# Experts' rests at fixed column counts in place of a choice among arms, in an attention, expert and dense kernel on one core

## The chip, the cores and the metric

One Trainium2 chip, one of its cores. The time is that of one execution of the program on the device, in microseconds. Of several runs the median is given. The engines are called as the profile calls them: PE (TensorE) for matrix products, PEld for its loading of weights, DVE (VectorE), ACT (ScalarE), POOL (GpSimd) and SP (SyncE, which issues most transfers). [...]

## What is computed

Three layers one after the other, in float32, on 2 x 768 tokens of 512 features:

```python
x = attention(q, k, v)                # windows of 16 and block summaries, 8 heads of 64
do_compute = x @ w_skip > 0           # tokens that fail this keep x
e_idx = argmax(x @ w_gate)            # one of 8 experts for each token
for e in range(8):
    mask = do_compute & (e_idx == e)
    h = maximum(x[mask] @ w1[e], 0)   # 512 -> 1024
    x[mask] += gate_w[mask] * (h @ w2[e])   # 1024 -> 512
h = x @ w_in                          # 512 -> 2048
out = (P(h) / Q(h)) @ w_out           # a ratio of polynomials, 2048 -> 512
```

How many tokens an expert gets is known only when the kernel runs.

## The kernel before

The kernel has three stages. The first is attention; while it runs, SP already loads the weights of experts 0, 1 and 2 (`PREFETCH`), 2 MB for each of `w1` and `w2`, into three pairs of buffers. It ends with the routing: tokens are sorted by expert, so that the tokens of an expert are neighbouring columns, and DVE writes each expert's first and last column, the starts of its windows (`regs`) and the limits of its masks (`lim`).

The second is the expert stage, of which the change speaks. Its instructions stand in an order written out by hand for PE, ACT, DVE, POOL and SP (L1050 to L1148); each engine works through its own in that order. POOL gathers the sorted tokens in 12 groups (L764), PE turns each group (`turned`, L1032), and ACT and DVE copy it to `xs`, which has 512 features on 4 x 128 partitions and 1536 columns. Then every expert has two parts:

- its *first*: the first 32 columns (`SMALL`). DVE builds a mask and a gated copy `xw` (`take_first`); PE computes in four steps, hidden (`th`, L810), turn (`tt`, L825), parts (`tp`, L833) and the sum over four groups (`ty`, L998 or L847), with an ACT copy between each two; DVE adds the result (`ysum`, `add_first`).
- its *rest*: the columns beyond 32. Only places 0, 1, 2 and 3 have one in the main order. Places 0 to 2 are the experts 0 to 2; at place 3 (`STAY`) stands whichever of the experts 3 to 7 has most tokens, which `choose` finds on DVE, and the others follow it. DVE masks and copies a window of 224 columns (`CAP`, `take_rest`) and clears a PSUM tile (`room`). PE and ACT read an index from a register (`arms_of`, with a hint to the sequencers) and go through one of eleven arms of a `Switch` (L980): none, 32 columns by the four steps of a first, or 64 to 224 columns by `large`, 64 products for the hidden layer (L783) and 64 for the output (L789). DVE then adds all 224 columns (`update`, L879).

The arms that this data takes can be read from the profile: none at place 0, 112 columns at place 1, 152 at place 2, 32 at place 3. What an expert has beyond its window is the business of a general part, under `tc.If(left > 0)` (L1152), which loads all experts' weights again and loops over windows of 224 columns; `left` is the greatest number of columns that are left over, worked out at the end of `choose`.

PSUM tiles of the firsts come from one pool of three buffers (`ps_t`), the output of a rest from a pool of one (`ps_y`). The weights of the experts at places 3 to 7 are loaded by SP into the three pairs in turn (`fetched`, L1014), each as soon as PE has used up what was there. Between these parts stand, in the same order, steps of a decoder (`decoder.steps`): it loads pieces of the dense stage's weights, 512 KB each, which DVE decodes in three operations (L719, L723, L725) and POOL splits in two (L737, L739), as far as buffers are free.

The third is the dense stage, again by hand: products of 128 x 128 with 512 columns, with DVE, ACT and POOL on the polynomials, and the rest of the decoding. Its first product stands at L1225.

Of the kernel before, what the change touches and what calls it, by code (L numbers as in the profile page):

```python
# [11 lines left out]
F32 = mybir.dt.float32  # L12
# [6 lines left out]
ALU = mybir.AluOpType  # L19
AX = mybir.AxisListType  # L20
ET = mybir.EngineType
PSUM = bass.MemoryType.PSUM

P = 128
B, H, S, D = 2, 8, 768, 64
N = B * S
DM = H * D
E = 8
# [4 lines left out]
CAP = 224  # L33
# [20 lines left out]
STAY = 3  # L54
# [12 lines left out]

PREFETCH = (5, 9, 15, 17, 20, 22)
SMALL = 32
ARMS = (0, 32, 64, 112, 128, 144, 152, 160, 176, 192, 224)  # L70
KC = DM // P


def shape_constants():

    mask = np.full((P, 3, 120), 1e9, np.float32)
    for n, t in enumerate((0, 1, S // 64 - 1)):
        for p in range(P):  # L80
            i = 64 * t + p % 64
            for c in range(96):
                j = 64 * t - 16 + c
                if 0 <= j < S and abs(i - j) < WIN:
                    mask[p, n, c] = 0.0
        mask[:, n, 96:] = -np.float32(np.log(BLK))

    avg = np.zeros((P, 7, 24), np.float32)
    for j in range(7):
        for p in range(P):  # L90
            s = 128 * j - 16 + p
            if 0 <= s < S:
                avg[p, j, s // BLK] = 1.0 / BLK

    ints = np.zeros((P, 316 + 304), np.float32)
    ints[:, 0:128] = np.arange(128)
    ints[:, 128:140] = 128.0 * np.arange(12)
    ints[:, 140:152] = np.arange(128)[:, None] + 128.0 * np.arange(12)
    ints[:, 152:161] = (8, 7, 6, 5, 4, 3, 2, 1, 0)
    ints[:, 168:296] = np.triu(np.ones((P, P), np.float32), 1)  # L100
    ints[:, 296:305] = np.tile(np.eye(32, 9), (4, 1))
    ints[:, 305:315] = np.add(ARMS[:-1], 0.5)
    ints[:, 316:572] = np.arange(256)
    ints[:, 572:604] = np.tile(np.eye(32), (4, 1))
    ints[:, 604:614] = np.add(ARMS[:-1], 0.5)
    return np.concatenate([mask.reshape(P, 360), avg.reshape(P, 168)], 1), ints


# [1 line left out]
def tile_kernel(ctx, tc, q, k, v, w_skip, w_gate, w1, w2, w_in, w_out, pa, pb, ma_d, ints_d, out):  # L110
    nc = tc.nc
# [10 lines left out]
    wts = {}  # L122
# [27 lines left out]
    routed = []  # L150
# [8 lines left out]
    def attention(c, io, wk, ps_s, ps_q, ps_t, ps_o):  # L159
# [468 lines left out]
        for n in range(3):  # L628
# [10 lines left out]


        rf = const.tile([P, 72], F32, name="rf")
        flag = const.tile([P, E, len(ARMS) - 1], F32, name="flag")
        nc.vector.tensor_copy(rf[:, 0:9], pb_)
        off, end = rf[:, 0:8], rf[:, 1:9]
        cnt, arm, win, most, fst, sec = (rf[:, 16 + 8 * i : 24 + 8 * i] for i in range(6))
        nc.vector.tensor_tensor(cnt, end, off, ALU.subtract)

        nc.vector.tensor_scalar(sec, off, float(SMALL), None, ALU.add)
        nc.vector.tensor_scalar(win, sec, float(N - CAP), None, ALU.min)
        nc.vector.tensor_scalar(fst, off, float(N - SMALL), None, ALU.min)  # L650
        nc.vector.tensor_tensor(lim[:, 3, :], end, win, ALU.subtract)
        nc.vector.tensor_tensor(lim[:, 0, :], off, fst, ALU.subtract)
        nc.vector.tensor_scalar(gate_s[:], pg[:], 1.0 / 16384.0, None, ALU.mult)
        nc.vector.tensor_tensor(
            flag[:],
            lim[:, 3, :, None].to_broadcast(flag.shape),
            ints[:, None, 305:315].to_broadcast(flag.shape),
            ALU.is_gt,
        )
        nc.vector.tensor_tensor(lim[:, 1, :], end, fst, ALU.subtract)  # L660
        nc.vector.tensor_reduce(arm, flag[:], AX.X, ALU.add)
        nc.vector.tensor_tensor(lim[:, 2, :], sec, win, ALU.subtract)
        nc.vector.tensor_copy(regs[:, 8:16], arm[0:1])
        nc.vector.tensor_copy(regs[:, 0:8], win[0:1])
        nc.vector.tensor_copy(regs[:, 40:48], fst[0:1])
        routed.extend([(off, end, cnt), rf[:, 24:40]])

    with ExitStack() as s_:
        pools = [
# [88 lines left out]
    with ExitStack() as s_:  # L758
# [97 lines left out]
        def reg(eng, i, top):  # L856
            return eng.value_load(i if not isinstance(i, int) else regs[:, i : i + 1], min_val=0, max_val=top)

        def masked(n, off, lo, hi, tg):

            win = bass.ds(off, n) if not isinstance(off, int) else slice(off, off + n)
            mg = mw.tile([P, CAP], F32, tag="mg", name=f"mg{tg}")
            pos = late_ints[:, 0:n]
            nc.vector.scalar_tensor_tensor(mg[:, :n], pos, lo, gate_b[:, win], ALU.is_ge, ALU.mult)
            if hi is not None:
                nc.vector.scalar_tensor_tensor(mg[:, :n], pos, hi, mg[:, :n], ALU.is_lt, ALU.mult)
            return n, win, mg

        def gated(mask, x):


            n, win, mg = mask
            nc.vector.tensor_tensor(
                x[:, :, :n], xs[:, :, win], mg[:, None, :n].to_broadcast([P, KC, n]), ALU.mult
            )
# [2 lines left out]
            win = bass.ds(off, n) if not isinstance(off, int) else slice(off, off + n)  # L878
            nc.vector.tensor_tensor(xs[:, :, win], py[:, :, :n], xs[:, :, win], ALU.add)  # L879

        arms = {}

        def arms_of(e, which):


            engs = {ET.PE: nc.tensor, ET.Activation: nc.scalar}
            index = {et: reg(eng, which, len(ARMS) - 1) for et, eng in engs.items()}
            arms[e] = index, tc.switch_hint(index, len(ARMS), f"rest{e}")

        def choose():  # L890


# [5 lines left out]
            def t_(name, shape, dt=F32):  # L898
                return mw.tile([P, *shape], dt, name=name)

            key, own, best, ge = t_("key", [n]), t_("own", [n]), t_("best", [1]), t_("ge", [n - 1])
            table, new, step, each = t_("table", [3, n]), t_("new", [3, n]), t_("step", [3, n - 1]), t_("each", [3, n])
            left, flag2, win = t_("left", [E]), t_("flag2", [len(ARMS) - 1]), t_("winx", [1])
            number = late_ints[:, STAY:E]
            nc.vector.scalar_tensor_tensor(key[:], cnt[:, late], float(E), number, ALU.mult, ALU.subtract)
            nc.vector.tensor_reduce(best[:], key[:], AX.X, ALU.max)
# [18 lines left out]
            nc.vector.tensor_tensor(lim[:, 1, late], end2, first_, ALU.subtract)  # L925
            yield

            nc.vector.tensor_scalar(win[:], off2[:, 0:1], float(SMALL), float(N - CAP), ALU.add, ALU.min)
            nc.vector.tensor_copy(pick[:, 1:2], win[0:1])
            nc.vector.tensor_scalar(key[:, 0:1], off2[:, 0:1], float(SMALL), None, ALU.add)  # L930
            nc.vector.tensor_tensor(lim[:, 2, STAY : STAY + 1], key[:, 0:1], win[:], ALU.subtract)
            nc.vector.tensor_tensor(lim[:, 3, STAY : STAY + 1], end2[:, 0:1], win[:], ALU.subtract)
            nc.vector.tensor_scalar(flag2[:], late_ints[:, 288:298], lim[:, 3, STAY : STAY + 1], None, ALU.is_lt)
            nc.vector.tensor_reduce(best[:], flag2[:], AX.X, ALU.add)
            nc.vector.tensor_copy(pick[:, 0:1], best[0:1])
            yield

            nc.vector.tensor_scalar(more[:, :STAY], off[:, :STAY], float(SMALL + CAP), None, ALU.add)
            nc.vector.tensor_scalar(more[:, late], off2, float(SMALL), None, ALU.add)
            nc.vector.tensor_scalar(  # L940
                more[:, STAY : STAY + 1], more[:, STAY : STAY + 1], float(CAP), None, ALU.add
            )
            nc.vector.tensor_copy(ends[:, :STAY], end[:, :STAY])
            nc.vector.tensor_copy(ends[:, late], end2)
            yield
# [4 lines left out]
            nc.vector.tensor_copy(pick[:, 3:4], best[0:1])  # L950

        xw = mw.tile([P, E, KC, SMALL], F32, name="xw")
        small, xr, py_first, py_rest, off_first, off_rest = [], {}, {}, {}, {}, {}

        def take_first(e):
            which = 40 + e if e < STAY else pick[:, 9 + e - STAY : 10 + e - STAY]
# [2 lines left out]
            return lambda: gated(mask, xw[:, e])  # L959

        def take_rest(e):
            xr[e] = mw.tile([P, KC, CAP], F32, tag="xr", name=f"xr{e}", bufs=2)
            off = off_rest[e] = reg(nc.vector, pick[:, 1:2] if e == STAY else e, N - CAP) if e else SMALL
            lo, hi = lim[:, 2, e : e + 1], lim[:, 3, e : e + 1]
            gated(masked(CAP, off, lo, hi, f"r{e}"), xr[e])

        def room(e):

            py_rest[e] = ps_y.tile([P, KC, 256], F32, tag="y", name=f"py{e}")
            nc.vector.memset(py_rest[e][:], 0.0)  # L970

        def first(e):
            small.append(Small(wts[e, 1], wts[e, 2], xw[:, e], str(e)))
            small[e].hidden()

        def rest(e):
            a, b_ = wts[e, 1], wts[e, 2]
            py = py_rest[e]
            index, hint = arms[e]
            for i in tc.Switch(index, len(ARMS), hint=hint):  # L980
                n = ARMS[i]
                if n == SMALL:
                    sm = Small(a, b_, xr[e], f"r{e}", ps_h)
                    for step in (sm.hidden, sm.turn, sm.parts):
                        step()
                    sm.total(py, 2)
                elif n:
                    large(a, b_, n, xr[e], py, f"r{e}_{i}")
            update(CAP, off_rest[e], py)

        def total_first(e):
            if e in DIRECT:
# [57 lines left out]
        with tc.manual_schedule(engines={ET.PE, ET.Activation, ET.DVE, ET.Pool, ET.SP}):  # L1050
# [8 lines left out]

            if G2:  # L1060
                gate_rows(2, 2)
            arms_of(0, 8)
            first(0)
            take_rest(0)
            room(0)
            if not G2:
                gate_rows(2, 2)
            turned(2)
            turned(3)
            places = choose()  # L1070
            next(places)
            rest(0)
            room(1)
            for t in range(4, NT):
                if t == TURN0:
                    small[0].turn()
# [15 lines left out]
            take_rest(1)  # L1092
            decoder.steps(*STEPS[0])

            arms_of(1, 9)
            first(2)
            small[1].turn()
            total_first(0)
# [3 lines left out]
            take_first(3)()  # L1102
            decoder.steps(*STEPS[1])
            rest(1)
            room(2)
            fetched(4, 2)
            for later in range(4, E):
                take_first(later)()
            decoder.steps(*STEPS[2])
            arms_of(2, 10)  # L1110
            small[2].turn()
            first(3)
            total_first(1)
# [5 lines left out]
            add_first(2)  # L1119
            decoder.steps(*STEPS[3])  # L1120
            rest(2)
            room(3)
            take_rest(3)
            fetched(5, 4)
            arms_of(3, pick[:, 0:1])
            first(4)
            total_first(3)
            small[4].turn()
# [276 lines left out]
```

## Time and profile before

| | us |
|---|---|
| three runs | 554.82, 557.14, 558.86 |
| median | 557.14 |
| the profiled execution | 556.66 |
| its span, first to last instruction | 554.9 |

The expert stage lies between some 95 and 245.9 us of the span; the routing's last operations stand at 95 to 96 us, and the first product of the dense stage at 245.9. Rows of the profile name a line of the kernel, an engine, an operation and the tiles as out<-in. A number in brackets behind a row of a timeline is the time that the engine stood idle ahead of it, with what ended the idle time; "issue" there means that the engine waited for nothing that the profile shows. [...] Records of the tool for branches of a `Switch` stand under the last line of the file, L1401.

### The profile page before, as it was taken

The page shows a single profiled execution, that of the slowest core. Times are in us where ns is not written, and L with a number is a line of the kernel's source. Part 1 is how long each engine was busy: PE and PEld are TensorE (multiplying, and loading weights), DVE is VectorE, ACT ScalarE, POOL GpSimd, SP SyncE. Part 2 cuts the span into 40 slices and gives each one's busy share as a digit, 9 for nine tenths or more (in the row PEclk, how much of TensorE's full clock was granted, in tenths as well). Part 3 has the DMA queues.
Part 4 walks back from the last instruction along what each step waited for, and adds up shares of the span by engine and source line. Part 5 has one row for each costly group of instructions (what it writes and reads, how often), then busy time and mean ns, then how long its engine had stood idle before and what let it go on. Part 6 is the DMA issues. An engine that isn't in the chain of part 4 may idle for free.

```text
span 554.9 us, 8712 instructions
## 1 busy us (share of the span) xinstructions
PE 466.9 (84%) x3127; PEld 348.3 (63%) x3127; DVE 409.5 (74%) x879; ACT 238.6 (43%) x455; POOL 198.3 (36%) x192
## 2 busy tenths in 40 slices
PE   8999998567868655787977787888999999999994
PEld 4677675344828422345756666567888887888872
DVE  4687678445984231858999999998787797887784
ACT  3565553131112010126444444626565676465650
POOL 2644400710345001635544444644322243322222
PEclk9999998678979887958999999989999999999998
DMA  9799971686393899222222222101000000100001
GB/s 288 219 370 353 402 234 73 183 284 217 133 342 107 292 322 377 85 80 76 76 76 77 76 77 76 38 2 58 20 0 1 0 2 38 38 1 0 2 0 76
DMA packets 28781, 71.67 MB, mean 129 GB/s; under 512 B 3040, under 2 KB 7072, under 8 KB 28704
## 3 DMA queue, kind: packets, MB, share of 16 engines
q1 hardware_dynamic: 24192, 55.26, 28.3%
q0 software_dynamic: 4368, 15.21, 8.1%
q8 instruction: 37, 0.61, 0.4%
q14 instruction: 40, 0.33, 0.2%
q10 hardware_dynamic: 144, 0.27, 0.1%
HBM read 64.44 MB, written 6.29 MB: 127 GB/s over the span
## 4 chain that ended last, share of the span: by engine, by line
PE 18%; DVE 17%; issue 13%; POOL 5%; ACT 2%; POOLq 0%; DVEq 0%; ACTq 0%
PE m L1225 10%; PE z L1283 8%; POOL t L1235 3%; DVE u L1264 2%; DVE t L1267 2%; DVE gh L1263 2%; DVE decwo L719 2%; DVE t L1239 2%; DVE decwi L719 2%; DVE decwi L723 1%; POOL out_dram L1308 1%; DVE decwo L725 1%; DVE gl L1268 1%; DVE decwo L723 1%; DVE decwi L725 1%
## 5 line engine op out<-in xcount | busy, mean ns | idle before, releaser
L1225 PE MATMUL m<-x,wi 128*128 128x512 f32 x576 | 146.2, 405 | 28.5 <-DVE gl L1268 25.9
L1225 PEld LDWEIGHTS m<-x,wi 128*128 128x128 f32 x576 | 110.5, 195 | 59.2 <-DVE gl L1268 29.7
L1235 POOL TENSOR_TENSOR t<-s,t 128x512 f32<-128x512 f32 x48 | 63.3, 1318 | 171.2 <-ACT s L1234 167.8
L1283 PE MATMUL z<-wo,gh 128*128 128x512 f32 x384 | 96.1, 389 | 0.0
L1232 ACT ACTIVATE t<-m,ab 128x512 f32<-128x512 f32 x48 | 37.4, 780 | 113.3 <-PE m L1225 113.3
L1283 PEld LDWEIGHTS z<-wo,gh 128*128 128x128 f32 x384 | 71.9, 188 | 15.2 <-POOL wo L739 0.3
L1283 PE MATMUL z<-wo,gl 128*128 128x512 f32 x192 | 52.6, 391 | 1.1 <-DVE gl L1268 1.1
L1263 DVE SCALAR_TENSOR_TENSOR gh<-t,ab,m 128x512 fp32r<-128x512 f32 (+1 forms) x51 | 36.4, 713 | 17.1 <-ACT m L1249 17.0
L1264 DVE SCALAR_TENSOR_TENSOR u<-t,c,gh 128x512 f32<-128x512 f32 (+1 forms) x51 | 39.3, 770 | 5.5 <-DVE gh L1263 0.5
L1283 PEld LDWEIGHTS z<-wo,gl 128*128 128x128 f32 x192 | 36.0, 188 | 9.8 <-DVE gl L1268 2.3
L1234 ACT ACTIVATE s<-t,absb 128x512 f32<-128x512 f32 x48 | 39.1, 815 | 4.4
L810 PE MATMUL th<-w,xw 128*32 128x256 f32 x256 | 24.2, 548 | 19.3 <-issue 11.1
L1267 DVE SCALAR_TENSOR_TENSOR t<-t,ab,u 128x512 f32<-128x512 f32 (+1 forms) x51 | 36.5, 716 | 1.8
L1239 DVE TENSOR_TENSOR t<-t,m 128x512 f32<-128x512 f32 x48 | 32.8, 684 | 6.1 <-ACT t L1233 5.1
L1268 DVE TENSOR_TENSOR gl<-t,m 128x512 fp32r<-128x512 f32 (+1 forms) x51 | 33.5, 656 | 4.8
L1243 DVE SCALAR_TENSOR_TENSOR t<-t,ab,m 128x512 f32<-128x512 f32 x48 | 35.8, 746 | 1.2
L299 ACT ACTIVATE tm<-tm,mx 128x120 f32<-128x120 f32 x96 | 29.9, 383 | 10.1 <-DVE mx L283 10.0
L1248 ACT ACTIVATE m<-t,c 128x512 f32<-128x512 f32 x48 | 32.3, 672 | 0.2 <-POOL t L1235 0.2
L810 PEld LDWEIGHTS th<-w,xw 128*32 128x32 f32 x256 | 11.3, 150 | 30.3 <-issue 19.2
L283 DVE CUSTOM_DVE_ANT_0 tm<-s,ma 128x120 f32<-128x120 f32 x96 | 21.3, 278 | 11.7 <-PE s L269 11.7
L1249 ACT ACTIVATE m<-m 128x512 f32<-128x512 f32 x48 | 27.9, 582 | 1.5
L1233 ACT ACTIVATE t<-m 128x512 f32<-128x512 f32 x48 | 28.4, 591 | 0.0
(217 smaller groups left out, 728.7 us busy)
## 6 DMA issues: line engine op xcount, KB each, us to landing
w<-in_moe_w_dram SPq DMA_DIRECT2D x16, 2048.0 KB, 11.1
rawwi<-in_moe_w_in_dram POOLq DMA_DIRECT2D x9, 512.0 KB, 4.8
rawwo<-in_moe_w_out_dram POOLq DMA_DIRECT2D x8, 512.0 KB, 4.0
rawwo<-in_moe_w_out_dram SPq DMA_DIRECT2D x8, 512.0 KB, 3.2
rawwi<-in_moe_w_in_dram SPq DMA_DIRECT2D x7, 512.0 KB, 3.5
kT<-in_k_dram SPq DMA_DIRECT2D x8, 400.0 KB, 6.6
ve<-in_v_dram SPq DMA_DIRECT2D x4, 780.0 KB, 7.1
qT<-in_q_dram SPq DMA_DIRECT2D x8, 384.0 KB, 7.9
```

The costliest lines, as they stand in the source:

```text
L810: nc.tensor.matmul(ph[SMALL * g : SMALL * g + SMALL], self.xw[:, c_, :SMALL], self.a[:, c_, 256 * g : 256 * g + 256], start=c_ == 0, stop= ...
L1225: nc.tensor.matmul(ph[:], w[:, l, c_, fs], x[c_][:, r], start=i == 0, stop=i == 3 * KC - 1)
L1232: nc.scalar.activation(t["t2"][:], ph[:], AF.Identity, scale=ab[:, 3:4], bias=ab[:, 2:3])
L1234: nc.scalar.activation(t["s2"][:], t["t1"][:], AF.Identity, scale=absb[:, 1:2], bias=absb[:, 0:1])
L1235: nc.gpsimd.tensor_tensor(t["t1"][:], t["s2"][:], t["t1"][:], ALU.mult)
L1239: nc.vector.tensor_tensor(t["t2"][:], t["t2"][:], ph[:], ALU.mult)
L1243: nc.vector.scalar_tensor_tensor(t["t2"][:], t["t2"][:], ab[:, 1:2], ph[:], ALU.add, ALU.mult)
L1263: nc.vector.scalar_tensor_tensor(gh[:, s], t2[:, s], ab[:, 0:1], r0[:, s], ALU.add, ALU.mult)
L1264: nc.vector.scalar_tensor_tensor(u[:, s], t1[:, s], c1[:, 0:1], gh[:, s].bitcast(F32), ALU.add, ALU.mult)
L1267: nc.vector.scalar_tensor_tensor(t2[:, s], t2[:, s], ab[:, 0:1], u[:, s], ALU.add, ALU.subtract)
L1268: nc.vector.tensor_tensor(gl[:, s], t2[:, s], r0[:, s], ALU.mult)
L1283: nc.tensor.matmul(zs[s4][:], l[:, P * s4 : P * s4 + P], w[:, r, f % 4, :], start=i == 0 and n in starts, stop=i == 2 and n in ends,)
```

## The change

The arms go. Each place has a fixed number of columns for its rest, `REST`: none at place 0, 128 at place 1, 160 at place 2, 32 at place 3 (by the four steps of a first), none behind. The columns that an expert doesn't fill are masked, as the surplus of an arm was; what it has beyond its fixed number is the general part's, whose test (`more`, `left`) is worked out from the new numbers. With the arms go the registers and hints for them, the flags from which DVE counted the index, the clearing of the PSUM tile (the products of a rest now start their own sums), and the whole rest of place 0 with its mask, copy and update. Masks, gated copies and updates take the fixed number of columns in place of 224. The order by hand is otherwise what it was.

```diff
@@ -67,7 +67,8 @@
 SMALL = 32
-ARMS = (0, 32, 64, 112, 128, 144, 152, 160, 176, 192, 224)
+
+REST = (0, 128, 160, 32, 0, 0, 0, 0)
@@ -99,10 +100,10 @@
-    ints[:, 305:315] = np.add(ARMS[:-1], 0.5)
+    ints[:, 305:313] = np.subtract(N, REST)
...
-    ints[:, 604:614] = np.add(ARMS[:-1], 0.5)
+    ints[:, 604:612] = np.add(SMALL, REST)
@@ -639,31 +640,22 @@
...
-        nc.vector.tensor_scalar(win, sec, float(N - CAP), None, ALU.min)
+        nc.vector.tensor_tensor(win, sec, ints[:, 305:313], ALU.min)
...
-        nc.vector.tensor_tensor(
-            flag[:],
-            lim[:, 3, :, None].to_broadcast(flag.shape),
-            ints[:, None, 305:315].to_broadcast(flag.shape),
-            ALU.is_gt,
-        )
         nc.vector.tensor_tensor(lim[:, 1, :], end, fst, ALU.subtract)
-        nc.vector.tensor_reduce(arm, flag[:], AX.X, ALU.add)
         nc.vector.tensor_tensor(lim[:, 2, :], sec, win, ALU.subtract)
-        nc.vector.tensor_copy(regs[:, 8:16], arm[0:1])
...
@@ -878,15 +870,6 @@
-        arms = {}
-
-        def arms_of(e, which):
-
-
-            engs = {ET.PE: nc.tensor, ET.Activation: nc.scalar}
-            index = {et: reg(eng, which, len(ARMS) - 1) for et, eng in engs.items()}
-            arms[e] = index, tc.switch_hint(index, len(ARMS), f"rest{e}")
-
@@ -925,21 +908,16 @@
-            nc.vector.tensor_scalar(win[:], off2[:, 0:1], float(SMALL), float(N - CAP), ALU.add, ALU.min)
+            nc.vector.tensor_scalar(win[:], off2[:, 0:1], float(SMALL), float(N - REST[STAY]), ALU.add, ALU.min)
...
-            nc.vector.tensor_scalar(flag2[:], late_ints[:, 288:298], lim[:, 3, STAY : STAY + 1], None, ALU.is_lt)
-            nc.vector.tensor_reduce(best[:], flag2[:], AX.X, ALU.add)
-            nc.vector.tensor_copy(pick[:, 0:1], best[0:1])
-            yield
-
-            nc.vector.tensor_scalar(more[:, :STAY], off[:, :STAY], float(SMALL + CAP), None, ALU.add)
-            nc.vector.tensor_scalar(more[:, late], off2, float(SMALL), None, ALU.add)
-            nc.vector.tensor_scalar(
-                more[:, STAY : STAY + 1], more[:, STAY : STAY + 1], float(CAP), None, ALU.add
-            )
+            yield
+
+            done = late_ints[:, 288 : 288 + E]
+            nc.vector.tensor_tensor(more[:, :STAY], off[:, :STAY], done[:, :STAY], ALU.add)
+            nc.vector.tensor_tensor(more[:, late], off2, done[:, late], ALU.add)
...
@@ -959,34 +937,27 @@
         def take_rest(e):
+            n = REST[e]
             xr[e] = mw.tile([P, KC, CAP], F32, tag="xr", name=f"xr{e}", bufs=2)
-            off = off_rest[e] = reg(nc.vector, pick[:, 1:2] if e == STAY else e, N - CAP) if e else SMALL
+            off = off_rest[e] = reg(nc.vector, pick[:, 1:2] if e == STAY else e, N - n) if e else SMALL
             lo, hi = lim[:, 2, e : e + 1], lim[:, 3, e : e + 1]
-            gated(masked(CAP, off, lo, hi, f"r{e}"), xr[e])
-
-        def room(e):
-
-            py_rest[e] = ps_y.tile([P, KC, 256], F32, tag="y", name=f"py{e}")
-            nc.vector.memset(py_rest[e][:], 0.0)
+            gated(masked(n, off, lo, hi, f"r{e}"), xr[e])
...
         def rest(e):
-            a, b_ = wts[e, 1], wts[e, 2]
-            py = py_rest[e]
-            index, hint = arms[e]
-            for i in tc.Switch(index, len(ARMS), hint=hint):
-                n = ARMS[i]
-                if n == SMALL:
-                    sm = Small(a, b_, xr[e], f"r{e}", ps_h)
-                    for step in (sm.hidden, sm.turn, sm.parts):
-                        step()
-                    sm.total(py, 2)
-                elif n:
-                    large(a, b_, n, xr[e], py, f"r{e}_{i}")
-            update(CAP, off_rest[e], py)
+            n = REST[e]
+            py = ps_y.tile([P, KC, 256], F32, tag="y", name=f"py{e}")
+            if n == SMALL:
+                sm = Small(wts[e, 1], wts[e, 2], xr[e], f"r{e}", ps_h)
+                for step in (sm.hidden, sm.turn, sm.parts):
+                    step()
+                sm.total(py, 2)
+            else:
+                large(wts[e, 1], wts[e, 2], n, xr[e], py, f"r{e}")
+            update(n, off_rest[e], py)
@@ -1059,18 +1030,13 @@
-            arms_of(0, 8)
             first(0)
-            take_rest(0)
-            room(0)
...
-            rest(0)
-            room(1)
...
-            arms_of(1, 9)
...
             rest(1)
-            room(2)
...
-            arms_of(2, 10)
...
             rest(2)
-            room(3)
             take_rest(3)
             fetched(5, 4)
-            arms_of(3, pick[:, 0:1])
```

## Rows read from the trace of the kernel before

**Rows 1.** The page: the span, and the busy time of each engine.

```profile
span 554.9 us, 8712 instructions
...
PE 466.9 (84%) x3127; PEld 348.3 (63%) x3127; DVE 409.5 (74%) x879; ACT 238.6 (43%) x455; POOL 198.3 (36%) x192
```

**Rows 2.** Stretches: start:end, length, engines' busy time (instructions), clock, DMA share, GB/s.

```profile
107.20:112.87 5.67, 1.03 (x9) 0.79 (x8) 3.68 (x11) 0.98 (x2) 4.75 (x6) 0.80 0.76 212
112.87:123.17 10.30, 9.41 (x58) 6.57 (x58) 3.87 (x18) 3.89 (x7) 0.17 (x1) 0.78 0.87 305
123.17:127.42 4.25, 0.01 (x1) 0.01 (x1) 2.93 (x17) 0.60 (x1) 0.00 (x0) 1.00 0.94 302
...
150.87:168.92 18.05, 10.04 (x77) 3.85 (x77) 15.65 (x28) 2.23 (x5) 9.15 (x11) 0.81 0.86 322
...
185.71:202.81 17.10, 6.66 (x55) 2.89 (x56) 8.78 (x13) 1.36 (x3) 1.13 (x2) 0.80 0.94 339
...
211.55:217.11 5.56, 0.00 (x2) 0.03 (x1) 1.09 (x1) 0.00 (x0) 0.00 (x0) 0.63 1.03 405
217.11:220.34 3.23, 3.23 (x33) 1.60 (x34) 0.00 (x0) 0.00 (x0) 0.00 (x0) 0.58 1.06 389
220.34:245.91 25.57, 18.19 (x143) 8.85 (x143) 16.40 (x19) 4.82 (x11) 15.76 (x18) 0.76 0.31 102
245.91:554.90 308.99, 273.01 (x1152) 218.29 (x1152) 263.75 (x365) 164.89 (x257) 115.11 (x98) 0.98 0.10 36
```

**Rows 3.** Timeline of PE: start, us, line, operation, count [idle before <-what ended it].

```profile
112.91 1.94 PE L1032 MATMUL xsT<-ident,xg 128*128 128x128 f32 x8 [4.68 <-issue]
...
191.22 3.64 PE L810 MATMUL th<-w,xw 128*32 128x256 f32 x32 [5.51 <-issue]
...
202.81 3.56 PE L810 MATMUL thr<-w,xr 128*32 128x256 f32 x32 [3.84 <-issue]
...
217.11 3.23 PE L810 MATMUL th<-w,xw 128*32 128x256 f32 x32 [5.56 <-issue]
...
223.61 1.91 PE L810 MATMUL th<-w,xw 128*32 128x256 f32 x32
...
238.23 3.64 PE L833 MATMUL tp<-w,hT 128*32 128x512 f32 x16 [0.54 <-ACT hT L827]
```

**Rows 4.** PE's groups by shape: count, busy us, mean ns, idle before.

```profile
L783 PE MATMUL phr<-xr,w 128*128 128x152 f32 x64 | 8.5, 294 | 2.0 <-issue 2.0
L789 PE MATMUL py<-hTr,w 128*128 128x152 f32 x64 | 8.4, 293 | 0.0
L783 PE MATMUL phr<-xr,w 128*128 128x112 f32 x64 | 7.7, 278 | 0.6 <-ACT hTr L786 0.6
L789 PE MATMUL py<-hTr,w 128*128 128x112 f32 x64 | 7.3, 275 | 0.0
```

**Rows 5.** Sequencer rows under L1401: count, ns min/median/max, first and last start.

```profile
L1401 PEldq COMPARE_BRANCH  x8: 311/4718/6474, 105.5 to 210.5; - x8
...
L1401 ACTq COMPARE_BRANCH  x8: 37/43/62, 108.4 to 209.8; - x8
```

**Rows 6.** The same view of L1152, the `If`.

```profile
L1152 PEldq COMPARE_BRANCH  x1: 5007/5007/5007, 227.0 to 227.0; - x1
```

**Rows 7.** The same view of L764, the gathers.

```profile
L764 POOL DMA_INDIRECT xg<-x_dram,idx x12: 942/946/1239, 96.7 to 110.9; - x12
```

**Rows 8.** DMA issues, whole run: count, KB each, median us to landing.

```profile
w<-in_moe_w_dram SPq DMA_DIRECT2D x16, 2048.0 KB, 11.1
...
xg<-x_dram,idx POOLq DMA_INDIRECT x12, 3.7
```

**Rows 9.** Timeline of all engines, 164 to 166 us.

```profile
164.19 0.68 DVE L1005 TENSOR_REDUCE ysum<-ty 128x128 f32<-128x512 f32 x1
...
164.43 0.66 PE L998 MATMUL ty<-ident,yp 128*128 128x128 f32 x4 [0.42 <-ACT yp L843]
```

**Rows 10.** Timeline of all engines, 170 to 340 us: SP's issues of weights.

```profile
182.12 29.83 SPq L1014 DMA_DIRECT2D w<-in_moe_w_dram  x6
```

More of the change, by code (lines that the diff above doesn't have):

```diff
@@ L641, in attention @@
         rf = const.tile([P, 72], F32, name="rf")
-        flag = const.tile([P, E, len(ARMS) - 1], F32, name="flag")
         nc.vector.tensor_copy(rf[:, 0:9], pb_)
         off, end = rf[:, 0:8], rf[:, 1:9]
-        cnt, arm, win, most, fst, sec = (rf[:, 16 + 8 * i : 24 + 8 * i] for i in range(6))
+        cnt, _, win, _, fst, sec = (rf[:, 16 + 8 * i : 24 + 8 * i] for i in range(6))
         nc.vector.tensor_tensor(cnt, end, off, ALU.subtract)
         nc.vector.tensor_scalar(sec, off, float(SMALL), None, ALU.add)
-        nc.vector.tensor_scalar(win, sec, float(N - CAP), None, ALU.min)
+        nc.vector.tensor_tensor(win, sec, ints[:, 305:313], ALU.min)
         nc.vector.tensor_scalar(fst, off, float(N - SMALL), None, ALU.min)
@@ L653, in attention @@
         nc.vector.tensor_scalar(gate_s[:], pg[:], 1.0 / 16384.0, None, ALU.mult)
-        nc.vector.tensor_tensor(
-            flag[:],
-            lim[:, 3, :, None].to_broadcast(flag.shape),
-            ints[:, None, 305:315].to_broadcast(flag.shape),
-            ALU.is_gt,
-        )
         nc.vector.tensor_tensor(lim[:, 1, :], end, fst, ALU.subtract)
-        nc.vector.tensor_reduce(arm, flag[:], AX.X, ALU.add)
         nc.vector.tensor_tensor(lim[:, 2, :], sec, win, ALU.subtract)
-        nc.vector.tensor_copy(regs[:, 8:16], arm[0:1])
         nc.vector.tensor_copy(regs[:, 0:8], win[0:1])
         nc.vector.tensor_copy(regs[:, 40:48], fst[0:1])
-        routed.extend([(off, end, cnt), rf[:, 24:40]])
+        routed.append((off, end, cnt))
     with ExitStack() as s_:
@@ L902, in choose @@
             table, new, step, each = t_("table", [3, n]), t_("new", [3, n]), t_("step", [3, n - 1]), t_("each", [3, n])
-            left, flag2, win = t_("left", [E]), t_("flag2", [len(ARMS) - 1]), t_("winx", [1])
+            left, win = t_("left", [E]), t_("winx", [1])
             number = late_ints[:, STAY:E]
@@ L952, in tile_kernel @@
         xw = mw.tile([P, E, KC, SMALL], F32, name="xw")
-        small, xr, py_first, py_rest, off_first, off_rest = [], {}, {}, {}, {}, {}
+        small, xr, py_first, off_first, off_rest = [], {}, {}, {}, {}
         def take_first(e):
```

## The prediction

> **What bounds the kernel now.** I read the page first. The span is 554.9 us and TensorE (PE) is busy for 84% of it [rows 1], which says little, because the kernel has several stages with different limits. So the second view is the table of stretches, cut at the edges of the PE's work in the expert stage [rows 2]. Its last line is the dense stage behind the experts: 308.99 us that the change doesn't touch. The lines above it are uneven: of 17.10 us in 185.71 to 202.81 PE is busy for 6.66, of 5.56 us in 211.55 to 217.11 for none. DVE, ACT and POOL aren't full in these two either, and what moves at 339 and 405 GB/s is weights for later experts.
>
> The third view is the timeline of PE, with what ended each idle time [rows 3]. Its holes lie at the edges of the four `Switch`es. Behind each of them stands one, 4.68 us at place 0 and 5.5 to 5.6 at the others; 3.84 us lie ahead of place 3, and the rows by shape have 2.0 ahead of place 2 and 0.6 inside the rest of place 1 [rows 4]. That is some 28 us. All but the 0.6 are put down to "issue": PE waited for nothing that the profile shows. The sequencers' own rows give the reason [rows 5]: the eight branches of PE took 4.7 us in the median and up to 6.5, those of ACT 43 ns. The one branch of `If`, which the change leaves in, took PE 5.0 us [rows 6], in another part of the code, which bears the price out. So in the expert stage PE's instruction stream is the bound wherever a branch stands, not a datum.
>
> **The change, part by part.** I follow PE's path through the stage. The profiled execution took 556.66 us, 1.8 us over its span; the sum goes against that. The median of the runs shown, 557.14, is 0.5 above.
>
> *Place 0.* The switch, the two masks, the gated copy and the update of the rest go, and nothing replaces them, since 0 columns are set. PE waited for none of it there. The hole of 4.65 us between the last turn at 108.2 and the next at 112.87 closes. [...] What is late next are the gathers: the last is issued at 110.9 [rows 7] and a gather lands 3.7 us later [rows 8], at 114.6; my end of the turns, about 117, lies behind it. The three flag operations in `choose`, small ones ahead of the last copy, go as well (0.55 us, an estimate from DVE's 2.93 us for 17 such operations in 123.17 to 127.42). The 4.25 us of DVE's chain ahead of expert 1 [rows 2] stay. Gain 6.6; ends 4.65 (the hole alone) and 8.2 (the gathers' limit, 123.17 - 115.6, with the flags).
>
> *Columns.* The two rests take 7.7 + 7.3 = 15.0 us at 112 columns and 8.5 + 8.4 = 16.9 at 152 [rows 4], 0.0475 us a column. 16 more and 8 more cost 0.76 + 0.38 = 1.14 us. The bounds are 0 (the weights' load sets the pace) and 1.9 + 0.4 (128 columns priced as 152). The wait of 0.6 us inside the first rest goes, since it follows ACT's own branch. Loss 0.6.
>
> *From the rest of place 1 to that of place 2.* [...] With 0.4 for ACT's short steps the stretch becomes 8.5: gain 9.5. What could be late next is DVE, busy for 15.65 us there [rows 2]. Does PE need it? In this kernel the transposition at 164.43 starts, on ACT's result, while DVE's sum of expert 1 still runs until 164.87 [rows 9], so it isn't held by DVE's release of a PSUM buffer. If in the new order some step of PE does wait for that sum, the stretch takes 14.0 (164.87 - 150.87) plus the last products, about 2: gain 2. Upper end 10.1. The DVE operations that go here (a memset, wider masks and copies) shorten DVE's chain a little and stay hidden.
>
> *From the rest of place 2 to that of place 3.* 17.10 us, of which 6.66 work at a clock of 0.80: 5.3, with 0.8 for ACT's steps 6.1. Gain 11.0; ends 9.35 (the two holes alone) and 11.5. DVE must update and mask the next rest in that time, some 3 us, and is ready before PE asks.
>
> *Place 3 and behind it.* The rest of 32 columns stays; its first 32 matmuls took 3.56 us [rows 3] and should take 1.91: gain 1.65. The hole of 5.56 behind it goes but for the register load that all engines do for `If`. I leave 0.35 of it; at most 0.9, by which this hole is longer than the first one, behind which no load stood. Gain 5.2, and 1.3 for the next 32 matmuls (3.23 to 1.91 us).
>
> *Behind that.* From 220.34 to the dense stage, 25.57 us, the work is the same: two more experts, DVE's and POOL's decoding, the branch of `If`, the last expert. The question is whether the weights come in time. Six transfers are issued from 182.12 on [rows 10], and the last product needs the last of them at 238.23 [rows 3]: 56 us. The change takes 11.0 + 1.65 + 5.2 + 1.3 = 19.2 from that: 37 us are left. Six times 2.1 MB at the 389 and 405 GB/s of two full stretches [rows 2] is 32 us, two pieces for the decoder 2.7, and the start of a transfer some 2: 37. So a cover of 19 us becomes none. I take 2.5 us lost here; ends 0 and 6 (one whole transfer late). Where a weight is late, DVE's and POOL's decoding, queued behind it, moves as well.
>
> **Sum.** 6.6 - 0.6 + 9.5 + 11.0 + 1.65 + 5.2 + 1.3 - 2.5 = 32.15. 556.7 - 32.2 = 524.5 us. A branch taken out of DVE, SP and POOL I cost at nothing: none of theirs stalled PE. `If` keeps its price.
>
> [...]
>
> **The rivals.**
> *DVE takes PE's place between the rests of places 1 and 2*: gain 2 there for 9.5. For it: DVE is the fullest engine there, and its chain doesn't shrink. Against it: rows 9. Time 524.5 + 7.5 = 532. Chance 0.2.
> *The weights become the bound* from expert 5 on, beyond my 2.5 us, because the transfers and the decoder's pieces share the DMA for 37 us. For it: zero cover; against it: the earliest transfer may start sooner, when the last matmul on the old weights ends. Loss up to two transfers more, 5 to 10 us: 530 to 535. Chance 0.13.
> [...] Chance 0.06.
> *The branch isn't what PE waits for*: the holes stay, the columns cost 1.1: 557 to 558. Against it: rows 5. Chance 0.03.
> *Slower: an expert has more tokens than its fixed place.* Then `If` is entered, and it loads all eight experts again into one pair of buffers: 16 transfers of at least 5.3 us and, one waiting for the other, of 11.1 [rows 8], 85 to 178 us, so 610 to 700. It decides from 129, 161 and 33 tokens on, beyond the first 32, at places 1, 2 and 3, and from 33 tokens at the others. Against it: the arms of the trace are 112, 152 and 32 columns [rows 4, 3], which hold the rests of these same tokens, place 0 took the empty arm, and the 16 weight loads of the whole run [rows 8] are those of the first pass alone, so no other expert has a rest. Chance 0.02.
>
> **How the numbers follow.** My forecast has 0.56. Its own ends, not all at once, give 518 to 530. The rivals of DVE, the weights and straight code reach 532 to 535, singly; two of them together 540. The range 517 to 539 leaves out the last two rivals and the tails. About 1%, 5.6 us, is what a measurement of this kernel can tell from no change. Faster by more: 0.95, all cases but the last two; within 1%: 0.03; slower: 0.02.
>
> **What would show it.** In the profile after, no branch of PE may stand between 105 and 200 us but that of `If`, at about 5 us. The stretch between the rests of places 1 and 2 should be near 8.5 us; if it is 14 to 16 with PE waiting for DVE's `ysum`, the first rival holds. That between the rests of places 2 and 3 should be near 6, the granted clock near 1.0 in both. The first matmul of the dense stage should start near 213 us instead of 245.9, and the rest should be the same 309 us. Idle PE ended by a DMA on `w` behind expert 5 would show the second rival. The forecast is wrong if the holes stay without branches, or if the dense stage grows.

## The result, and the profile after

The kernel after takes 522.62 us in the median of 4 runs (521.46 to 523.28), beside 557.07 of before (554.82 to 558.86): a ratio of 0.942, with an interval of 0.937 to 0.947. The 557.07 is the median of the three runs shown before and a fourth, 557.0. Ratios and intervals here come from the fast runs alone, those within 1.5% of the fastest of the same kernel, and needn't be the quotient of the medians, which are over all runs. The profiled execution took 521.46 us, with a span of 519.7. That of before was 554.9, so 35.2 us are to be found in the two spans. From here on "after" is the kernel with the change. Lines have moved: L810 is now L802, L833 is L825, L783 and L789 are L775 and L781, and the `If` is L1113.

The head of the page after, beside [rows 1]. The kernel executes fewer instructions, and PE is busy for 88% instead of 84%.

```profile
span 519.7 us, 8562 instructions
PE 455.6 (88%) x3127; PEld 342.1 (66%) x3127; DVE 395.4 (76%) x864; ACT 238.9 (46%) x455; POOL 198.2 (38%) x192
```

The table of stretches of after, cut at the same pieces of work as [rows 2]. After the stretch and its length stand the busy times of PE, PE's weight loads, DVE, ACT and POOL with their counts, then the granted clock (the share of its full speed that PE was granted on average), the DMA share and GB/s.

```profile
96.68:106.69 10.01, 5.90 (x44) 3.28 (x45) 1.46 (x8) 1.64 (x4) 7.32 (x8) 0.66 0.55 156
106.69:114.62 7.93, 7.67 (x66) 5.36 (x62) 4.77 (x23) 4.54 (x9) 5.45 (x7) 1.00 0.76 211
114.62:119.96 5.34, 0.63 (x4) 0.42 (x5) 2.75 (x17) 0.79 (x2) 0.00 (x0) 0.96 0.98 346
119.96:127.79 7.83, 7.79 (x86) 3.42 (x87) 6.16 (x12) 1.04 (x3) 0.72 (x2) 0.81 1.03 398
127.79:142.25 14.46, 14.46 (x133) 14.46 (x130) 10.23 (x15) 2.82 (x9) 4.71 (x6) 1.00 0.68 245
142.25:150.03 7.78, 7.43 (x77) 2.89 (x76) 6.53 (x14) 1.75 (x4) 5.21 (x6) 1.00 0.94 330
150.03:167.65 17.62, 17.62 (x136) 17.45 (x134) 13.17 (x20) 3.03 (x9) 8.99 (x11) 1.00 0.77 273
167.65:172.76 5.11, 4.58 (x55) 2.07 (x58) 4.37 (x9) 0.77 (x2) 1.28 (x2) 1.00 0.89 290
172.76:179.93 7.17, 5.35 (x66) 2.57 (x62) 2.47 (x4) 1.97 (x4) 1.14 (x2) 1.00 1.04 406
179.86:181.79 1.93, 1.93 (x34) 1.00 (x34) 0.29 (x1) 0.00 (x0) 0.00 (x0) 1.00 1.02 408
181.79:211.52 29.73, 18.27 (x144) 7.67 (x143) 13.64 (x19) 4.83 (x11) 16.26 (x18) 0.77 0.80 303
211.52:519.70 308.18, 272.19 (x1152) 217.61 (x1152) 263.13 (x365) 164.94 (x257) 114.53 (x98) 0.98 0.11 36
```

Read it from the middle. The stretch from the rest of place 1 to that of place 2 (142.25 to 150.03) takes 7.78 us instead of 18.05, with 77 matmuls in both and PE busy for all but 0.35 us. The next of that kind (167.65 to 172.76) takes 5.11 us instead of 17.10. From 127.79 to 181.79 the granted clock is 1.00 in every line; before it was 0.58 to 0.81 behind the holes [rows 2]. The line that grew most is the last but one: 29.73 us for 25.57. The rest of place 2 (150.03 to 167.65) grew by 0.83.

The timeline of PE after, as [rows 3]: start, us, line, operation, count and, in brackets, the idle time before it and what ended it.

```profile
118.32 0.63 PE L1003 MATMUL xsT<-ident,xg 128*128 128x128 f32 x4 [3.70 <-DMA xg<-x_dram,idx]
119.96 2.36 PE L802 MATMUL th<-w,xw 128*32 128x256 f32 x20 [1.01 <-DVE xw L865]
...
147.59 0.66 PE L969 MATMUL ty<-ident,yp 128*128 128x128 f32 x4 [0.35 <-ACT yp L835]
...
172.76 1.91 PE L802 MATMUL thr<-w,xr 128*32 128x256 f32 x32
...
179.86 1.93 PE L802 MATMUL th<-w,xw 128*32 128x256 f32 x32
...
190.67 3.12 PE L825 MATMUL tp<-w,hT 128*32 128x512 f32 x16 [2.47 <-SPq L1113]
198.39 3.44 PE L802 MATMUL th<-w,xw 128*32 128x256 f32 x32 [4.59 <-SPq L1113]
...
204.96 3.57 PE L825 MATMUL tp<-w,hT 128*32 128x512 f32 x16 [1.87 <-SPq L1113]
...
211.52 3.91 PE L1186 MATMUL m<-x,wi 128*128 128x512 f32 x9 [1.14 <-issue]
```

The holes put down to "issue" in the expert stage are gone, and the 32 matmuls that took 3.23 to 3.64 us behind one take 1.91 and 1.93. Three new waits stand near the end, 8.93 us in sum. The profile puts them down to SP's sequencer at L1113, but what SP has there are nine semaphore records of 17 ns each and a branch of 53; the experiment `two_less` below shows that the transfers of weights set them.

The one branch that PE still makes between 105 and 200 us, in the sequencers' rows (count, ns min/median/max, first and last start), as [rows 6]. A name with a q behind it, as PEldq, stands for the rows of that engine's sequencer:

```profile
L1113 PEldq COMPARE_BRANCH  x1: 6170/6170/6170, 190.7 to 190.7; - x1
```

Three stretches of before, in the same columns, that [rows 2] leave out: the first products of places 1 and 2, the rest of place 1 and the rest of place 2.

```profile
127.42:135.52 8.10, 8.00 (x87) 3.73 (x87) 6.77 (x12) 1.16 (x3) 0.53 (x1) 0.79 0.43 158
135.52:150.87 15.35, 14.79 (x132) 14.44 (x128) 11.64 (x16) 2.49 (x9) 5.55 (x7) 1.00 0.40 130
168.92:185.71 16.79, 16.79 (x128) 16.56 (x128) 3.85 (x5) 2.38 (x8) 5.51 (x7) 1.00 0.36 110
```

Term by term against the forecast, from the two tables of stretches (us gained, a loss negative; "routing" is the stage ahead of the experts, whose end slid from 95.61 to 96.68 in the profiled execution):

| part | forecast | measured |
|---|---|---|
| routing ends later | – | -1.07 |
| place 0, from there to place 1's first product | 6.6 | 31.81 - 23.28 = 8.53 |
| place 1's and 2's first products | – | 8.10 - 7.83 = 0.27 |
| the two wider rests | -0.6 | (15.35 - 14.46) + (16.79 - 17.62) = 0.06 |
| rest 1 to rest 2 | 9.5 | 18.05 - 7.78 = 10.27 |
| rest 2 to rest 3 | 11.0 | 17.10 - 5.11 = 11.99 |
| rest 3 | 1.65 | 8.74 - 7.17 = 1.57 |
| exit of the last switch | 5.2 | 5.56 - (179.86 - 179.93) = 5.63 |
| next 32 matmuls | 1.3 | 3.23 - 1.93 = 1.30 |
| tail up to the dense stage | -2.5 | 25.57 - 29.73 = -4.16 |
| dense stage | 0 | 308.99 - 308.18 = 0.81 |
| sum | 32.15 | 35.2 |

### The profile page after: what moved, and what is told of

Read it like the earlier page. It is cut to its first block, busy times and chain, and to the rows that moved or that the text cites. A ratio compares the mean times of both kernels' runs of the same rounds, so it can differ in the third digit from the quotient of the medians.

```text
span 519.7 us, 8562 instructions
## 1 busy us (share of the span) xinstructions
PE 455.6 (88%) x3127; PEld 342.1 (66%) x3127; DVE 395.4 (76%) x864; ACT 238.9 (46%) x455; POOL 198.2 (38%) x192
## 4 chain that ended last, share of the span: by engine, by line
DVE 19%; PE 18%; issue 15%; POOL 5%; ACT 2%; POOLq 0%; DVEq 0%; ACTq 0%
PE m L1186 9%; PE z L1244 8%; POOL t L1196 4%; DVE u L1225 3%; DVE t L1228 2%; DVE gh L1224 2%; DVE decwo L711 2%; DVE decwi L711 2%; DVE t L1200 2%; DVE decwo L717 1%; POOL out_dram L1269 1%; DVE decwo L715 1%; DVE decwi L717 1%; DVE decwi L715 1%; DVE gl L1229 1%
## 5 line engine op out<-in xcount | busy, mean ns | idle before, releaser
L1186 PEld LDWEIGHTS m<-x,wi 128*128 128x128 f32 x576 | 109.3, 193 | 59.1 <-DVE gl L1229 30.1
L1225 DVE SCALAR_TENSOR_TENSOR u<-t,c,gh 128x512 f32<-128x512 f32 (+1 forms) x51 | 37.4, 733 | 5.1
L270 PE MATMUL s<-kW,qT 64*64 64x120 f32 x384 | 25.3, 272 | 0.4 <-issue 0.4
L802 PE MATMUL th<-w,xw 128*32 128x256 f32 x256 | 19.3, 456 | 5.7 <-SPq L1113 4.6
```

The lines of the kernel that those rows point to most:

```text
L1186: nc.tensor.matmul(ph[:], w[:, l, c_, fs], x[c_][:, r], start=i == 0, stop=i == 3 * KC - 1)
L1225: nc.vector.scalar_tensor_tensor(u[:, s], t1[:, s], c1[:, 0:1], gh[:, s].bitcast(F32), ALU.add, ALU.mult)
```

## Experiment 1: only the branches are taken out

The kernel before, its four `Switch`es replaced by the arm that these inputs take. With them go the register loads and hints that chose the arm (`arms_of`). Everything else of before stays: masks of 224 columns, the memset, place 0's mask, gated copy and update, rests of 112, 152 and 32 columns.

```diff
-            index, hint = arms[e]
-            for i in tc.Switch(index, len(ARMS), hint=hint):
-                n = ARMS[i]
-                if n == SMALL:
-                    ...
-                elif n:
-                    large(a, b_, n, xr[e], py, f"r{e}_{i}")
+            n = (0, 112, 152, SMALL)[e]
+            if n == SMALL:
+                ...
+            elif n:
+                large(a, b_, n, xr[e], py, f"r{e}")
```

> The kernel before with the four Switches alone taken out: each rest is straight code of the arm that this data takes (none, 112, 152, 32 columns). Masks and updates stay 224 wide, PSUM is still cleared, and the rest of place 0 is still masked and added on DVE. It computes the reference for this data and no other. Theory 1, PE's branches were the whole gain: no branch of PE but If's, near the changed kernel, 521 to 526 us (0.8 us less for 152 columns in place of 160, up to 3 more for DVE's work at place 0 and the wider masks). Theory 2, the fixed columns and DVE's lighter work gave much of it: 530 to 550 us.

Measured: 526.28 us (524.52 to 528.2, 4 runs), ratio 0.946 (0.940 to 0.952). Theory 1 expected 521 to 526. So 30.7 of the 34.45 us of the change come with the branches and what feeds them. What is left for all the rest of the edit is 3.7 us between the medians, and the two intervals overlap.

Two of its stretches, in the columns of the table above: place 0, from routing's end to place 1's first product, and the tail.

```profile
96.42:121.67 25.25, 15.39 (x110) 9.41 (x111) 15.12 (x60) 7.08 (x14) 12.92 (x14) 0.80 0.70 224
182.84:216.08 33.24, 18.91 (x144) 8.51 (x143) 13.20 (x19) 4.82 (x11) 15.74 (x18) 0.71 0.76 290
```

Place 0 takes 25.25 us where after takes 23.28 (10.01 + 7.93 + 5.34). The work of place 0's empty rest that is still there has that size: its update took DVE 1.08 us and the memset behind it 0.91, in the middle of the copies that the turns need. The tail is 3.5 us longer than that of after for the same work. The first of its last six weights was issued at 160.50 instead of 159.02, and PE's waits for weights in it add up to 11.9 us for 8.93, four of them for three. Three are put down to SP, as in after; at the additional one the profile names the weight itself:

```profile
187.38 1.93 PE L810 MATMUL th<-w,xw 128*32 128x256 f32 x32 [1.07 <-DMA w<-in_moe_w_dram]
```

Why more of it is lost than the 1.5 us of the later start, I didn't settle.

The groups of PE by shape in the straight kernel (count | busy us, mean ns | idle before), beside [rows 4], where the same 64 matmuls at 112 columns took 7.7 us:

```profile
L783 PE MATMUL phr<-xr,w 128*128 128x152 f32 x64 | 8.5, 294 | 0.0
L789 PE MATMUL py<-hTr,w 128*128 128x152 f32 x64 | 8.4, 293 | 0.0
L783 PE MATMUL phr<-xr,w 128*128 128x112 f32 x64 | 7.4, 276 | 0.0
L789 PE MATMUL py<-hTr,w 128*128 128x112 f32 x64 | 7.3, 275 | 0.0
```

And the same view of after, at 160 and 128 columns:

```profile
L775 PE MATMUL phr<-xr,w 128*128 128x160 f32 x64 | 9.0, 301 | 0.0
L781 PE MATMUL py<-hTr,w 128*128 128x160 f32 x64 | 8.9, 299 | 0.0
L775 PE MATMUL phr<-xr,w 128*128 128x128 f32 x64 | 7.4, 277 | 0.0
L781 PE MATMUL py<-hTr,w 128*128 128x128 f32 x64 | 7.3, 275 | 0.0
```

112 and 128 columns cost the same 14.7 us; from 152 to 160 the 128 matmuls go from 16.9 to 17.9, about 0.1 us a column. The cost isn't a straight line through 112 and 152: it is the same at 112 and 128, and rises from there to 152 and 160.

## Experiment 2: the branches put back, with nothing to skip

Does each branch cost, or only one that has to jump over ten other arms? This kernel is the one after, with a `Switch` of two arms around each of the three rests: arm 0 is empty, arm 1 is the rest, and arm 1 is always taken. The register loads, the hints and the clearing of the PSUM tile come back with them, so the experiment doesn't separate these from the branches.

```diff
-            if n == SMALL:
-                ...
+            index, hint = arms[e]
+            for i in tc.Switch(index, 2, hint=hint):
+                if not i:
+                    continue
+                if n == SMALL:
+                    ...
```

> The changed kernel with a Switch of two arms put back around the rests of places 1, 2 and 3: arm 0 is empty, arm 1, the last one, holds the fixed columns, and a register that always says 1 chooses; PSUM is cleared as before. Theory A, a branch of PE costs some 5 us wherever it leads: three entries and three exits come back, 0.6 + 2.0 + 3.8 ahead and 5.5 behind each, some 23 us, plus 4 to 5 for the clock, less the 4 that the late weights take in the changed kernel: 543 to 549 us. Theory B, only the way over the code of the other arms costs: the last arm ends where the code goes on, so its exits are free and the entries lead over a few instructions: 523 to 529 us.

Measured: 550.9 us (548.85 to 557.33, 10 runs), ratio 0.994 (0.989 to 0.998). Three switches with empty alternatives take back 28 of the 34.45 us by the medians, some 29 by the two ratios (0.994 and 0.942). Theory B, 523 to 529 us, falls; theory A, 543 to 549, was 2 us too low at its upper end. The sequencers' rows of it:

```profile
L1384 PEldq COMPARE_BRANCH  x6: 391/3342/4764, 125.1 to 205.5; - x6
L1384 ACTq COMPARE_BRANCH  x6: 37/43/62, 126.9 to 204.8; - x6
```

The six branches of PE are at most 5 x 4.76 + 0.39 = 24.2 us, less than what is lost, and the timeline of PE shows why the rows of the branches don't hold the whole price:

```profile
148.16 3.64 PE L803 MATMUL th<-w,xw 128*32 128x256 f32 x32
...
168.39 8.86 PE L782 MATMUL py<-hTr,w 128*128 128x160 f32 x64
179.75 1.06 PE L803 MATMUL th<-w,xw 128*32 128x256 f32 x13 [2.51 <-DVE mgr L859]
185.20 2.77 PE L803 MATMUL th<-w,xw 128*32 128x256 f32 x19 [4.39 <-issue]
...
205.47 1.08 PE L840 MATMUL py<-late_ints,ypr 128*128 128x32 f32 x8 [0.76 <-ACT ypr L836]
206.48 1.50 PE L803 MATMUL th<-w,xw 128*32 128x256 f32 x23
211.79 1.49 PE L803 MATMUL th<-w,xw 128*32 128x256 f32 x9 [3.82 <-issue]
```

One part is the clock. The 32 matmuls at 148.16, behind a hole of 3.94 us, took 3.64 us, as they do at 191.22 in the kernel before, where the granted clock is 0.50 from 192 to 194 us; in after they took 1.93, at 1.00. Another isn't a branch's stall at all: the 2.51 us ahead of 179.75 are put down to DVE, which clears a PSUM tile again ahead of that (a memset that took it 0.91 us at 187.13 in the kernel before).

Behind the last branch, at 205.5, PE goes on at once: that one is the 391 ns of the row. But 23 matmuls later it stands for 3.82 us with nothing to wait for, in the middle of a loop of 32 that ran without a hole in after (179.86). The same after 13 matmuls at 180.81. So it seems that the stall of a branch can come a while behind it, where the row of the branch shows little: at these two places PE stands for 4.39 and 3.82 us without any datum missing that the profile shows. The profile lists queues of the kind "instruction", and they moved packets in both holes, 180.81 to 185.20 and 207.98 to 211.79:

```profile
q8 instruction: 1, 0.02, 1.5%
...
q8 instruction: 1, 0.02, 2.0%
```

Over the whole run q8 moved 37 packets in the kernel before, 26 in after and in the straight kernel, and 34 here, so the kernels with branches moved more of them. For which engine a packet was the profile doesn't say, and none of these runs shows that its landing ended the hole.

## Experiment 3: more code to skip

As experiment 2, with two more arms, never taken, of 128 matmuls each behind the one that is.

```diff
-            for i in tc.Switch(index, 2, hint=hint):
+            for i in tc.Switch(index, 4, hint=hint):
                 if not i:
                     continue
+                if i > 1:
+                    large(wts[e, 1], wts[e, 2], 64 * i, xr[e], py, f"r{e}_{i}")
+                    continue
```

> As switch2, with two more arms behind the one that is taken, each 128 products of 128 or 192 columns that never run. PE must go over some 500 instructions at each exit. Theory A (every branch costs): 543 to 549 us, as switch2. Theory B (the way over code costs): three exits of some 5.5 us and their clock come back and the entries don't: 536 to 543 us, some 14 more than switch2.

Measured: 555.17 us (547.8 to 562.26, 10 runs), ratio 0.993 (0.989 to 0.998), the same ratio as with two arms, each to within 0.0045, some 2.5 us. The medians alone lie 4 us apart. Theory B, some 14 us more than experiment 2, doesn't hold; theory A again was too low, by 6 us. The rows of the branches:

```profile
L1387 PEldq COMPARE_BRANCH  x6: 1876/4485/6140, 127.4 to 207.3; - x6
```

Their median is higher (4485 ns for 3342) and the short one is gone, but the profiled execution is one of the longest here, 557.5 us, so nothing is built on that. A few us for the further jump aren't excluded. But the bulk, 28 us, is there with almost nothing to jump over: what costs here is that there is a branch, far more than how much code it skips.

## Experiment 4: two transfers less at the end

The kernel after, without the loads of the second weights for places 6 and 7. The products there take the weights of places 4 and 3 instead, so this kernel computes something else.

```diff
             for k, w, shape in ((1, w1, [P, KC, FF]), (2, w2, [P, FF // P, DM])):
+                if e > 5 and k == 2:
+                    wts[e, 2] = wts[e - (2 if e == 6 else 4), 2]
+                    continue
```

> The changed kernel without two of its transfers: the second weights of the experts at places 6 and 7 are not loaded, the products take those of places 4 and 3 instead, so the output isn't the reference's. Theory 1, the weights' arrival sets the stretch from place 5 to the dense stage (29.7 us, where 25.6 were): PE's waits for weights at the last products go and the stretch is 25 to 26 us: 518 to 519 us. Theory 2, the branch of If (6.2 us on PE) or DVE's decoding sets it: no change, 522 to 523 us.

Measured: 516.6 us (515.98 to 517.62, 4 runs), ratio 0.929 (0.924 to 0.934): 6 us less than after, where theory 1 expected 518 to 519. Its tail as a stretch, then in its timeline and sequencers' rows:

```profile
180.51:205.36 24.85, 17.72 (x143) 8.14 (x143) 16.22 (x19) 4.83 (x11) 17.25 (x18) 0.79 0.57 196
```

```profile
192.70 3.64 PE L802 MATMUL th<-w,xw 128*32 128x256 f32 x32 [3.66 <-PEq L1116]
```

```profile
L1116 PEldq COMPARE_BRANCH  x1: 4999/4999/4999, 187.2 to 187.2; - x1
```

The three waits of 8.93 us are gone with the two transfers, so transfers set them. What comes to light is the hole of the `If`'s branch, 3.66 us, as in the kernel before:

```profile
232.55 2.82 PE L810 MATMUL th<-w,xw 128*32 128x256 f32 x32 [3.69 <-PEq L1152]
```

In after that branch took 6.17 us, from 190.7 to 196.9, and is hidden: PE waited for the weight behind it until 198.39.

Why the weights bind can be read from what the DMA moved in after, from the first of the last six loads (159.02) to the last product that needs them (204.96). First the stretch, then bytes and issues of the same window:

```profile
159.02:204.96 45.94, 34.04 (x327) 20.05 (x326) 25.16 (x35) 6.54 (x15) 23.62 (x28) 0.89 0.98 368
```

```profile
DMA packets 5877, 16.93 MB, mean 368 GB/s; under 512 B 226, under 2 KB 226, under 8 KB 5867
...
w<-in_moe_w_dram SPq DMA_DIRECT2D x6, 2048.0 KB, 16.6
rawwi<-in_moe_w_in_dram POOLq DMA_DIRECT2D x4, 512.0 KB, 5.5
rawwo<-in_moe_w_out_dram POOLq DMA_DIRECT2D x4, 512.0 KB, 8.3
```

The DMA is full, with a share of 0.98 over the whole 45.94 us, and besides the six weights it carries eight pieces for the decoder. A weight takes 16.6 us to land in the median there, 11.1 over the whole run of before [rows 8].

## Why the prediction was right, and where its terms were off

The forecast was 524.5 us in a range of 517 to 539; 522.62 came. Its reason was right: where PE's branches stood, they were the bound, and no datum. Experiment 1 takes the branches away and has 30.7 of the 34.45 us; experiment 2 puts three of the four switches back and loses 28. That the number came within 2 us is luck in part: single terms are off by up to 1.9 us one way and 1.7 the other, and cancel in part.

**The two stretches between the rests, the exit, rest 3** hold 29.5 of the 35.2 us (forecast 27.35). The step that the same matmuls run at the full clock where no hole stands ahead of them was right: 1.91 to 1.93 us for 32, clock 1.00. In the kernel before, the 32 at 191.22, behind a hole, took 3.64 us and those at 223.61, without one, 1.91 [rows 3]; the clock then, in the columns of the tables of stretches:

```profile
192.00:194.00 2.00, 2.00 (x24) 1.13 (x20) 0.00 (x0) 0.00 (x0) 0.00 (x0) 0.50 1.06 399
...
224.00:226.00 2.00, 2.00 (x34) 1.07 (x24) 1.97 (x3) 0.90 (x2) 0.73 (x1) 1.00 0.01 4
```

The surplus of 0.8 and 1.0 us in the two stretches is for the most part PE's own work, 7.43 and 4.58 us, for which the forecast had taken 8.1 and 5.3, their 10.04 and 6.66 us of work times the mean clock, 0.81 and 0.80, of stretches that had holes in them [rows 2]. No run shows the 8.1 that the forecast's 8.5 rests on; after shows 7.43, at a clock of 1.00. The waits for ACT are 0.35 and 0.53 us, where it had set 0.4 and 0.8.

**The rival of DVE falls.** PE waits for no result of DVE between the rests, although DVE is busy for 6.53 of 7.78 us there. Its work there was 15.65 us before; a good part now runs beside the rest of place 2, where DVE went from 3.85 us of work to 13.17.

**Place 0** was mis-sized, by two errors of opposite sign. The turns were to gain 6.05 us of the 6.6, of which 4.65 are the hole and 1.4 an estimate for a fuller clock. No run shows the 1.4 by itself; the clock where the turns stand went from 0.78 [rows 2] to 1.00 (106.69 to 114.62). They gained 4.22, from 123.17 to 118.95 at their end, or 5.29 counted from routing's end, since the last gather landed late and PE stood 3.70 us for it (the timeline at 118.32). The chain of DVE behind the turns, 4.25 us, was to stay but for three flag operations. It shrank to 1.01: while PE waited for that gather, DVE did its small operations. The upper end, 8.2, was taken as the gathers' limit; the two together gave 8.53. That they belong together is seen in experiment 4, the same code up to here: there PE waited 0.16 us ahead of the last turns, the wait for DVE's `xw` was 3.20, and place 1 began at 118.47 instead of 119.96. What the gather shared the DMA with is on record: with the gap of place 0 gone, the first weights for place 3 are issued at 111.66 instead of 116.78, 0.42 us behind the last gather. In after 1.17 MB of the queue that carries the weights moved while that gather was under way, and it took 7.0 us to land, where the forecast took 3.7. In experiment 4 that load came 1.36 us behind the gather, 0.04 MB of it moved, and the gather took 4.3. That the load holds up the gather is read from these two executions, not tried.

**The columns** were priced by a slope that isn't there. The step that failed is the line from 112 to 152 columns: the two rows of 112 in the trace of before had 0.3 us more in them than the same matmuls have in straight code (15.0 for 14.7), and from 112 to 128 the columns cost nothing. So the first rest grew for nothing and lost that 0.3 and the wait of 0.6, the second grew by 0.8 to 1.0 us, and the two came out at 0.06. The bounds (0 to 2.3 of cost, 0.6 of gain) held it.

**The tail** is the term that was mis-sized on the losing side: 4.16 us for 2.5. The forecast left 37 us for the transfers, with the hole of `If` in them. Counted in the same way some 40.7 were there: 45.94 less the 8.93 of waiting, with 3.7 for that hole, which the waits cover. The gains ahead were larger than the forecast's, but the first of the six loads was issued 8.63 us ahead of the end of its rest (159.02 to 167.65), where it had been 3.59 (182.12 to 185.71). The need of 37 was too low: the forecast counted two pieces for the decoder where eight were issued in that window. Its 2 us for the start of a transfer fit the trace of before, where SP's eight loads of 512 KB for `rawwo` landed in 3.2 us in the median and 0.524 MB at 405 GB/s are 1.3. Six pieces of 0.524 MB more are 3.15 MB, at 368 GB/s 8.5 us, and 37 + 8.5 is 45.5, near the 45.94 that it took. Of the 8.93 us of waits 3.7 replaced the hole of `If`, which the forecast had left standing in full, and behind the last product's start 1.1 us came back (6.56 us to the dense stage for 7.68). So the rival of the weights did hold in its mechanism, but with 1.7 us beyond the 2.5 of the forecast where it had set 5 to 10. That the decoder's pieces alone are to blame was worked out, not tried.

**That PE stalls in straight code as well**, the rival at 0.06, falls: no hole with "issue" is left on PE between 119.96 and 198.39, at a DMA share of 0.68 to 1.04, though packets of the instruction queues still come (seven between 119.96 and 179.86). **That the branch isn't it** falls with experiments 1 and 2. ACT's branches under the switches took 37 to 62 ns [rows 5]; PE's shortest took 311 ns and most of them several us. **The general part** isn't entered: `If` takes its one branch, and there are no further loads of weights.

## What to carry to other kernels

Look at the sequencers' rows of a branch before its arms: on the engine that sets the end, six branches around three rests cost 28 us here, so masked work of a fixed size is the better bargain as long as the extra columns cost less than two stalls of 4 to 5 us (4.7 for a branch of PE in the median of [rows 5]), and here 128 columns cost what 112 do. The bargain holds for inputs that fit the fixed numbers, as these tokens do; an expert with more of them sends the kernel into the general part, which no run here entered and the forecast put at 610 to 700 us. When such holes go, add up all that the DMA has to move in the time that is left, the small transfers of other stages too; the forecast's cover of 19 us was gone at once, and the next bound was there. A wider first rest and an earlier start of the last loads would be the next things to measure on this kernel; neither has a number here.

## What the runs showed that I had not expected

- A hole need not stand right behind the branch: in experiment 2 PE ran 23 matmuls behind a branch of 391 ns and then stood for 3.82 us with nothing to wait for, and a packet of the instruction queue q8 fell into that hole.
- Two more arms of 128 matmuls each, never taken, change the ratio from 0.994 to 0.993: the length of the code that is skipped is worth a few us at most here.
- 64 matmuls of 128 rows in f32 take the same 7.3 to 7.4 us at 112 and at 128 columns, and 8.9 to 9.0 at 160.
- Taking out a hole seems to have held up something else: the weights of place 3, issued 5.1 us sooner, moved beside the last gather, which then took 7.0 us to land.
- A branch of 6.17 us, the only one left on PE in after's expert stage, was hidden, because a weight landed later still; with two transfers less the branch of `If` cost 3.66.
